# An S4D block with a gated feed-forward on one core: x kept on chip and normalised whole, gates folded into the magnitudes, the skip term added outside PE

## The chip, the cores and the metric

The kernel runs on one core of one Trainium2 chip. The metric is the device time of one execution in microseconds (us). Engines: PE multiplies matrices (PEld is its weight load), DVE, ACT and POOL work on vectors, SP issues the transfers. Each engine executes its own instructions strictly in order.

## The reference, cut to what matters

```python
L, D, N, F = 2048, 640, 128, 1728
mod = (silu(c) @ w_mod).reshape(c.shape[0], 6, 1, -1)
sa, ca, ga, sb, cb, gb = mod[:, 0], ..., mod[:, 5]
h = layernorm(x) * (1 + ca) + sa
dt = exp(log_dt); A = -exp(log_A_real) + 1j * A_imag
C = (C_real + 1j * C_imag) * dt[:, None]
K = 2.0 * einsum("dn,dnl->dl", C, exp((A * dt[:, None])[:, :, None] * arange(L))).real
y = irfft(rfft(h.T, 2 * L) * rfft(K, 2 * L))[:, :L].T + h * D_skip
x = x + ga * y
h = layernorm(x) * (1 + cb) + sb
x = x + gb * ((silu(h @ w1) * (h @ w3)) @ w2)
```

All is float32. The first half makes for each of 640 channels a convolution kernel of 2048 points out of 128 decaying oscillations, and convolves the normalised, modulated h with it by transforms. The second half is a gated feed-forward network.

## The kernel before, in words

The 640 channels are five blocks of 128 (b), each of eight chunks of 16 channels. For each of the forty chunks POOL adds phases (ph) from two small integer tables p and multiplies magnitudes (yy and xx out of e and x_e); ACT takes sines (tr); DVE makes five products of them (yy<-yy,tr and xx<-tr,xx, one of them 1024 wide); PE multiplies yy and xx into kps, which holds the convolution kernel of the chunk; ACT copies kps into ks (the rows). The tables p and step are begun twice per block, from pS, by `begin`: a shift by 0 to 4 bits into five places, on DVE for the very first, on POOL as a copy and four additions for the nine others. `al8` and `mag` prepare the exponentials per block; each may run on POOL or DVE.

The state h takes another way. x is loaded whole once (tiles xs) for its means and squares, then again in 64 KB pieces (xq), 128 channels by 4 rows of tokens at a time. `h_norm` scales and shifts such a piece into a PSUM tile hn (four instructions, on ACT or DVE), `h_mul` multiplies by the gate row rA, `h_add` adds rB and writes hb (both DVE, 512 wide), `h_store` sends hb to the scratch hs in HBM, and `h_fetch` brings it back turned, as xb. `fold` makes rA = (1+ca)*ga and rB = sa*ga out of the modulation rows rw. So ga is multiplied into h.

Both go through the same two transforms: the first on PE (ps<-wk,xb is h, task hh; ps<-wk,ks is the kernel, task k), copied to sp by ACT or DVE; the second, fh and fk, with the factors wb (2 MB); then DVE and ACT multiply the spectra (hq, fp, fk), PE makes the inverse transform fz, and zt is stored to zd. For blocks 1 to 4 the kernel's first transform already goes in chunk pairs: matmuls of 64 rows by 64 columns, in the four quadrants of the array. The skip term enters as the first matmul of each kps (kps<-dsk,ident). When all blocks are through, x and zd are gathered and the feed-forward part follows.

The order is written out by hand: every step is a task with a number, and `Plan.run` emits them in the order of the list ORDER, where a suffix a, d or p picks ACT, DVE or POOL for a task that leaves it open. Engines wait for each other by semaphores only. The line L147 in the profile is the helper that all of the first half is issued through; so its instructions are told apart by their tiles.

## Time and profile before

| what | us |
|---|---|
| median of 3 runs (lowest to highest) | 945.77 (945.37 to 947.55) |
| the profiled execution | 945.84 |
| its span, first to last instruction | 944.0 |
| PE busy, DVE busy | 849.6, 700.5 |
| ACT busy, POOL busy | 515.1, 346.4 |
| mean granted TensorE clock | 0.967 of full speed |

The span is what the profile resolves; 1.8 us lie around it. The busy times are sums over the whole span, and the first 376 us (the S4D half) and the rest (the feed-forward) have different limits, so the shares have to be read by stretch. A row of a group gives line, engine, operation, output<-inputs, sizes, count, then busy time in us, the mean in ns, and the idle time just ahead with what ended it.

### The profile page before, as it was taken

Reading aid. Unit: us, or ns where it says so; the run is one execution under the profiler, and the core shown is the slowest. Engines: PE = TensorE matmul, PEld = TensorE weight load, DVE = VectorE, ACT = ScalarE, POOL = GpSimd, SP = SyncE. Lnnn points to the kernel's source line nnn. Section 1 sums busy time; section 2 is a strip of 40 time slices with the busy share of each in tenths; the row PEclk is TensorE's granted clock in tenths of the full one; section 3 lists DMA queues with packets and bytes.
Section 4 is the critical chain, followed back from the end, with each engine's and each line's share of the span. In section 5 each row is a group of like instructions: output and inputs, shape, how many; then the busy total and the mean of one; then the engine's idle time right before and its main releaser. Section 6 shows DMA issues by size and latency. Waiting matters only on the chain.

```text
span 944.0 us, 22044 instructions
## 1 busy us (share of the span) xinstructions
PE 849.6 (90%) x8963; PEld 674.2 (71%) x8963; DVE 700.5 (74%) x1232; ACT 515.1 (55%) x886; POOL 346.4 (37%) x355
## 2 busy tenths in 40 slices
...
GB/s 244 241 255 126 170 147 170 48 104 103 27 124 40 177 149 232 254 182 153 151 64 146 84 161 77 111 84 70 42 84 70 57 50 48 38 77 111 77 149 82
DMA packets 124941, 112.78 MB, mean 119 GB/s; under 512 B 12328, under 2 KB 107048, under 8 KB 123560
## 3 DMA queue, kind: packets, MB, share of 16 engines
...
q10 hardware_dynamic: 768, 0.92, 0.4%
...
HBM read 90.38 MB, written 20.97 MB: 118 GB/s over the span
## 4 chain that ended last, share of the span: by engine, by line
PE 67%; DMA 10%; DVE 8%; ACT 6%; issue 3%; POOL 3%; SPq 1%; DVEq 0%; ACTq 0%; POOLq 0%
PE p L820 17%; PE acc L1067 16%; PE gu L1030 6%; PE gu L1032 6%; PE gu L1031 6%; PE ps L147 4%; PE fz L147 3%; DMA low<-zd 3%; PE kps L147 2%; PE fk L147 2%; DVE yy L147 2%; PE fh L147 2%; DVE fp L147 1%; DMA wq<-in_w 1%; ACT hn L147 1%
## 5 line engine op out<-in xcount | busy, mean ns | idle before, releaser
L1030 PE MATMUL gu<-xh,wh 128*128 128x512 f32 x270 | 106.2, 398 | 1.9 <-ACT xh L609 1.1
L1032 PE MATMUL gu<-xh,wl 128*128 128x512 f32 x270 | 105.4, 390 | 0.0
L1031 PE MATMUL gu<-xl,wh 128*128 128x512 f32 x270 | 105.2, 390 | 0.0
L147 ACT ACTIVATE tr<-ph 128x512 f32<-128x512 f32 (+1 forms) x160 | 92.9, 599 | 7.0 <-DVE yy L147 5.5
L839 POOL TENSOR_TENSOR ws<-wp 128x256 f32<-128x256 f32 x13 | 9.6, 739 | 230.9 <-DVE x L610 116.0
L147 POOL TENSOR_TENSOR ph<-p,p 128x1024 int32<-128x1024 int32 x40 | 78.2, 1955 | 3.0 <-ACT tr L147 2.7
L147 DVE TENSOR_TENSOR yy<-yy,tr 128x512 f32<-128x512 f32 (+1 forms) x80 | 75.4, 942 | 1.5 <-ACT tr L147 1.2
L723 ACT ACTIVATE wh<-wr 128x640 fp32r<-128x640 f32 x51 | 34.9, 731 | 70.5 <-PE gu L1031 55.6
L820 PE MATMUL p<-x,wch 128*128 128x512 f32 x208 | 68.3, 389 | 0.0
L1030 PEld LDWEIGHTS gu<-xh,wh 128*128 128x128 f32 x270 | 50.6, 188 | 18.3 <-issue 2.1
L147 PE MATMUL kps<-yy,xx 128*32 128x64 f32 x2560 | 49.3, 228 | 10.8 <-DVE xx L147 4.6
L1032 PEld LDWEIGHTS gu<-xh,wl 128*128 128x128 f32 x270 | 50.7, 188 | 11.2 <-DVE wl L733 0.4
L736 POOL MEMSET w2l<- 64x640 f32 x1 | 0.6, 631 | 157.8 <-PE acc L1067 157.8
L1031 PEld LDWEIGHTS gu<-xl,wh 128*128 128x128 f32 x270 | 50.7, 188 | 10.2 <-DVE xl L610 0.2
L147 DVE TENSOR_TENSOR xx<-tr,xx 128x512 f32<-128x512 f32 x80 | 54.3, 680 | 1.1 <-ACT tr L147 0.8
L857 DVE TENSOR_TENSOR s<-p,s 128x512 f32<-128x512 f32 x52 | 34.7, 682 | 27.0 <-ACT s L855 23.0
L147 POOL TENSOR_TENSOR yy<-e,e 128x512 f32<-128x512 f32 x48 | 52.7, 1109 | 4.5 <-PE kps L147 2.5
L147 PEld LDWEIGHTS kps<-yy,xx 128*32 128x32 f32 x2560 | 43.2, 113 | 11.6 <-POOL yy L147 4.5
L1045 DVE TENSOR_TENSOR a<-a,gu 128x512 f32<-128x512 f32 x26 | 17.8, 686 | 45.0 <-PE gu L1032 44.9
L1043 ACT ACTIVATE th<-gu 128x512 f32<-128x512 f32 x26 | 15.5, 596 | 64.3 <-PE gu L1032 64.3
L147 PE MATMUL ps<-wk,xb 128*64 128x128 f32 x640 | 47.1, 296 | 3.0 <-ACT sp L147 1.4
L147 PE MATMUL fh<-sp,wb 128*64 128x128 f32 x640 | 44.4, 284 | 4.9 <-DVE fp L147 2.2
...
## 6 DMA issues: line engine op xcount, KB each, us to landing
...
```

Source lines behind the costliest of these rows:

```text
L147: self.prev = self.k.order(f(*a, **kw), self.prev)
L723: self.nc.scalar.activation(wh[:, i], raw[:, i], AF.Copy)
L736: self.nc.gpsimd.memset(w2l[64:].bitcast(F32), 0.0)
L820: nc.tensor.matmul(to, t[:, o], y[:, k], start=start and k == i == 0, stop=stop and (k, i) == (n - 1, 2), skip_group_check=True)
L839: G.tensor_tensor(s[0], a21, a22, op=ALU.add)
L857: add = lambda o, bk, s: V.tensor_tensor(o, bk, s, op=ALU.add)
L1030: nc.tensor.matmul(pg, wh[:, k, :], xh[:, k, :], start=(k == 0), stop=False)
L1031: nc.tensor.matmul(pg, wh[:, k, :], xl[:, k, :], start=False, stop=False)
L1032: nc.tensor.matmul(pg, wl[:, k, :], xh[:, k, :], start=False, stop=(k == KT - 1))
L1043: nc.scalar.activation(th, gu[0], AF.Tanh, scale=0.5)
L1045: nc.vector.tensor_mul(a, a, gu[1])
L1067: nc.tensor.matmul(acc[k], *two(a, w), start=(m == 0 and i == 0), stop=(m == 12 and i == 2))
```

## The change

x is loaded once, ahead of the gates' weights, and stays on chip. Sixteen ACT instructions of 640 elements normalise it in place of the 80 small ones (each of the four tiles goes into the tile of the one before; the first into sp). The squares of the statistics are written to scratch so that x survives. The 80 loads of x in pieces disappear, and eight stores of 256 KB or 1 MB stand in place of 20 of 256 KB.

The gates are split: B = sa/(1+ca) is added to the normalised x, and A = (1+ca)*ga is multiplied into the magnitudes mag and the skip row dsk of blocks 1 to 4, which scales the convolution kernel in place of h. Block 0, whose magnitudes are needed early, still has A multiplied into x (`am`), then A*B added (`aa`), 512 wide; the other four blocks get one 2048-wide addition per tile of x (`ab`). Small column operations (`gates`) make A and B, and `gm`, `gd` multiply A into mag and dsk.

The skip matmuls disappear; ten `skip_add` instructions add dsk to the last column of ks. The first transform of h goes in chunk pairs too (`pair_tasks`): 64x64 quadrants. All ten `begin` are on DVE. The second half of w_mod is loaded in turn into the tiles of xb, wb and xs, and the load of the factors wb waits until these are used. In ORDER nearly all numbers change, since the tasks are others; three al8, mag and the like change engine there.

```diff
-1 2 8 7 12 78 80 3 79 86 81 41 14 19 82 20 42 84 21 15 83 43 85 16 153p 44 17 4 22 154 18 23 28 61 45 59 30 120 31 46 121 24
...
+1 2 5 78 3 80 4 6 81 20 14 82 19 41 84 21 7 15 42 8 22 83 16 9 11 190d 10 23 191 43 17 44 24 18 25 28 45 109 30 59 26 31 46 29
...
-            nc.scalar.activation(xs[:, j], xs[:, j], AF.Square, bias=self.h_nm[:, s], accum_out=self.h_ss[:, s])
+            nc.scalar.activation(self.rw[:, 0], xs[:, j], AF.Square, bias=self.h_nm[:, s], accum_out=self.h_ss[:, s])
...
-        def begin(e):
+        def begin():
 
             by = by_t(pS)
-            to = (p1[:, :, :, 1], by_t(st[:, 0]), by_t(st[:, 1]), p2[:, :, :, 1], by_t(st[:, 2]))
-            for i, d in enumerate(to):
-                if e == "DVE":
-                    V.tensor_scalar(d, by, i, None, op0=ALU.logical_shift_left)
-                elif i:
-                    add(d, to[i - 1], to[i - 1])
-                else:
-                    G.tensor_copy(d, by)
+            for i, d in enumerate((p1[:, :, :, 1], by_t(st[:, 0]), by_t(st[:, 1]), p2[:, :, :, 1], by_t(st[:, 2]))):
+                V.tensor_scalar(d, by, i, None, op0=ALU.logical_shift_left)
 
...
-        return [("DVE", .9, lambda: begin("DVE")) if b == h == 0 else ("POOL", 1.9, lambda: begin("POOL")),
+        return [("DVE", .9, begin),
...
-            b, c = d0 // P, d0 % P // C
-            last = kps.rearrange("p (e b) -> p e b", b=64)[:, :, 63]
-            for q in range(4):
-                s = slice(32 * q, 32 * q + 32)
-                nc.tensor.matmul(last[s], self.ident[:, s], self.dsk[:, b, 4 * c:4 * c + 4], start=True, stop=False,
-                                 tile_position=(0, 32 * q), skip_group_check=True)
...
-                                         start=False, stop=(r == 1), tile_position=(0, 32 * q), skip_group_check=True)
+                                         start=(r == 0), stop=(r == 1), tile_position=(0, 32 * q), skip_group_check=True)
...
-        plan.add("inv", None, 0, inv, ["cols", "mag1"], 0)
+        self.later = [f"k0.{x}.m" for x in range(6)] + ["colsf"]
+        self.stored = [f"{x}{i}" for x in ("as", "at") for i in range(4)]
+        plan.add("inv", None, 0, inv, ["cols", "mag1"] + self.stored, 0)
...
-            self.first_tasks(b, 0)
-            self.first_tasks(b, 1)
+            self.pair_tasks(b, 0)
+            self.pair_tasks(b, 1) if b else self.first_tasks(b)
...
-    def h_norm(self, pc, b, out, e):
-        x = self.xq[pc, b]
-        self.xq[pc, b] = out = out.rearrange("p (j d) -> p j d", j=4)
+    def h_parts(self, b):
+
+        x = self.xn[b].rearrange("p (k a j i) -> p k a j i", k=NB, a=4, j=4)
+        row = lambda r, k: bc(r[:, k.start * P:k.stop * P].rearrange("p (a i) -> p a i", i=E4), 2, 4)
+        return x, row
+
+    def h_norm(self, xs, b, j):
+
+        x, _ = self.h_parts(b)
         rstd, nb = self.h_rs
-        for j in range(4):
-            s = slice(4 * b + j, 4 * b + j + 1)
-            if e == "DVE":
-                self.nc.vector.tensor_scalar(out[:, j], x[:, j], rstd[:, s], nb[:, s], op0=ALU.mult, op1=ALU.add)
-            else:
-                self.nc.scalar.activation(out[:, j], x[:, j], AF.Identity, scale=rstd[:, s], bias=nb[:, s])
-
-    def h_mul(self, pc, b):
-        x = self.xq[pc, b]
-        self.nc.vector.tensor_tensor(x, x, bc(self.rA[:, pc * P:pc * P + P], 1, 4), op=ALU.mult)
-
-    def h_add(self, pc, b):
-
-        x = self.xq.pop((pc, b))
-        hb = self.hb[pc, b] = self.ring(f"hb{pc}{b}").rearrange("p (a j i) -> p a j i", a=4, j=4)
-        self.nc.vector.tensor_tensor(hb, x.rearrange("p j (a i) -> p a j i", a=4),
-                                     bc(self.rB[:, pc * P:pc * P + P].rearrange("p (a i) -> p a i", a=4), 2, 4), op=ALU.add)
-
-    def h_store(self, pc, b):
-        hb = self.hb.pop((pc, b))
-        self.nc.sync.dma_start(self.hs[pc, :, :, :, b, :].rearrange("a g t c -> (g t) a c"),
-                               hb.rearrange("p a j i -> p a (j i)"))
+        s = slice(4 * b + j, 4 * b + j + 1)
+        self.nc.scalar.activation(x[:, :, :, j].rearrange("p k a i -> p (k a) i"), xs[:, j].rearrange("p (k i) -> p k i", i=E4),
+                                  AF.Identity, scale=rstd[:, s], bias=nb[:, s])
+
+    def h_row(self, b, k, r, op, e):
+
+        x, row = self.h_parts(b)
+        v = x[:, k].rearrange("p k a j i -> p (k a) j i")
+        self.eng(e).tensor_tensor(v, v, row(r, k), op=op)
+
+    def h_store(self, b, k):
+
+        x, _ = self.h_parts(b)
+        to = self.hs[k].rearrange("k a g t b c -> b (g t) (k a) c")[b]
+        self.nc.sync.dma_start(to, x[:, k].rearrange("p k a j i -> p (k a) (j i)"))
...
-            add(n + "p", "PE", 1.1, lambda c=c: ch[c][4](), [n + f"m{i}" for i in range(5)] + (["dsk"] if b == 0 else []), t + 3,
+            add(n + "p", "PE", 1.1, lambda c=c: ch[c][4](), [n + f"m{i}" for i in range(5)], t + 3,
...
+            if c % 4 == 3:
+                add(f"d{b}.{c // 4}", ("POOL", "DVE"), (.28, .15), lambda e, h=c // 4: self.skip_add(b, h, e), [f"{g}.{x}.r" for x in range(c - 3, c + 1)] + (["gd"] if b else ["dsk"]), t + 3, port=True)
+    def skip_add(self, b, h, e):
+
+        to = self.ks[b][h][:, :, 63]
+        self.eng(e).tensor_tensor(to, to, self.dsk[:, b, 16 * h:16 * h + 16], op=ALU.add)
...
-            add(n + "n", ("ACT", "DVE"), (1.95, .85), lambda e, i=i, place=place: self.h_norm(b, i, place(), e), ...
-            add(n + "x", "DVE", .61, lambda i=i: self.h_mul(b, i), [n + "n", "fold"], t + .1)
-            add(n + "a", "DVE", .61, lambda i=i: self.h_add(b, i), [n + "x"], t + .2, take=[("hz", 1)], give=[(bank, n + "n")])
...
-            add("h0.f", "SP", 0, lambda: self.h_fetch(0), old, W["h"](b, 4), dma=[262144] * 4)
+            add("h0.f", "SP", 0, lambda: self.h_fetch(0), [f"as{i}" for i in range(4)] + ["mc0", "turn1"], W["h"](b, 4), dma=[262144] * 4)
...
-    def kernel_tasks(self, b):
+    def pair_tasks(self, b, m):
...
-                x = self.ks[b][i // 2][:, 8 * i % 16 + e, :]
+                x = self.ks[b][i // 2][:, 8 * i % 16 + e, :] if m else xb[:, :, 8 * i + e]
...
+        g = ("hh", "k")[m]
         for i in range(4):
+            t = W[g](b, 2 * i)
+            n = f"{g}{b}.{i}."
+            if m:
+                after = [f"g{b}.{2 * i}.r", f"g{b}.{2 * i + 1}.r", f"d{b}.{i // 2}"]
+            else:
+                after = [f"h{b}.f"] + (["wk"] + [f"mr{x}" for x in range(4)] + self.later if b == 0 else [])
+            old = [f"w{b - 1}.{x}.{'fk'[m]}" for x in range(8)] if b else []
...
+        def turn_cols():
+            pv = mt[1] = ps.tile([P, 512], F32, name="pvm", tag="f", bufs=3)
+            for o in range(4):
+                nc.tensor.matmul(pv[:, o:16:4], mt[0][:, o * P:(o + 1) * P], self.ident[:, 0:P:32], start=True, stop=True)
+
+        def gates():
+
+            pv = mt[1]
+            sa, ca, ga = (pv[:, k * KT:k * KT + KT] for k in range(3))
+            z, A, B, q = pv[:, 16:16 + KT], ab[:, :KT], ab[:, KT:2 * KT], ab[:, 2 * KT:]
+            V.tensor_scalar(q, ca, 1.0, None, op0=ALU.add)
+            V.scalar_tensor_tensor(z, q, -1.0, q, op0=ALU.mult, op1=ALU.max)
+            V.tensor_scalar(z, z, 1e-18, 4e-18, op0=ALU.is_lt, op1=ALU.mult)
+            V.tensor_tensor(q, z, q, op=ALU.add)
+            V.tensor_mul(A, q, ga)
+            V.reciprocal(q, q)
+            V.tensor_mul(B, sa, q)
+            V.tensor_mul(B[:, :1], B[:, :1], A[:, :1])
...
-        def fold():
-            self.rA, self.rB = self.rows[1], self.rows[0]
-            V.scalar_tensor_tensor(self.rA, self.rA, 1.0, self.rows[2], op0=ALU.add, op1=ALU.mult)
-            V.tensor_mul(self.rB, self.rB, self.rows[2])
-        add("fold", "DVE", 1.6, fold, [f"rw{g}" for g in range(4)], 22, port=True)
...
+        squares = [f"sq{b}{j}" for b in range(4) if b not in W["stat_v"] for j in range(4)]
+        for g in range(3):
+            add(f"pr{g}", "PE", .9, lambda g=g: spread(g), ["vc"], 21, take=[("f2", 1)])
+            add(f"rw{g}", "ACT", .5, lambda g=g: keep(g), [f"pr{g}", "lat1", "pa4"] + squares, 21, give=[("f2", f"pr{g}")])
+        rows = [f"rw{g}" for g in range(3)]
+        self.xn = [spf[:, :2560]] + [None] * 3
+        first, rest = slice(0, 1), slice(1, NB)
+
+        def norm(b, j):
+            if b and j == 0:
+                self.xn[b] = xs[b - 1].rearrange("p j d -> p (j d)")
+            self.h_norm(xs[b], b, j)
+        for b in range(4):
+            for j in range(4):
+                after = ["hscale", f"x{b}"] + ([f"n{b - 1}.{x}" for x in range(4)] if b else [f"mr{x}" for x in range(4)])
+                add(f"n{b}.{j}", "ACT", .74, lambda b=b, j=j: norm(b, j), after + ([f"n{b}.0"] if j else []), 22)
+            n = [f"n{b}.{j}" for j in range(4)] + rows
+            add(f"am{b}", ("POOL", "DVE"), (1.02, .6), lambda e, b=b: self.h_row(b, first, self.rA, ALU.mult, e), n, 22, port=True)
+            add(f"aa{b}", ("POOL", "DVE"), (1.02, .6), lambda e, b=b: self.h_row(b, first, self.rB, ALU.add, e), [f"am{b}"], 22, port=True)
+            add(f"as{b}", "SP", 0, lambda b=b: self.h_store(b, first), [f"aa{b}"], 22, dma=[262144])
+            add(f"ab{b}", ("POOL", "DVE"), (3.3, 2.25), lambda e, b=b: self.h_row(b, rest, self.rB, ALU.add, e), n, 22, port=True)
+            add(f"at{b}", "SP", 0, lambda b=b: self.h_store(b, rest), [f"ab{b}"], 22, dma=[262144] * 4)
+
+        def gate_sizes(e):
+
+            m = self.mag[:, 1:].rearrange("p b (e j) -> p b e j", j=4)
+            r = self.rA[:, P:].rearrange("p (b j e) -> p b e j", j=4, e=E4)
+            for k in range(NB - 1):
+                self.eng(e).tensor_tensor(m[:, k], m[:, k], r[:, k], op=ALU.mult)
+
+        def gate_skip(e):
+            for q in range(4):
+                s = slice(32 * q, 32 * q + 32)
+                d = self.dsk[s, 1:]
+                self.eng(e).tensor_tensor(d, d, self.rA[s, P:].rearrange("p (b q e) -> p b q e", q=4, e=E4)[:, :, q], op=ALU.mult)
+        add("gm", ("POOL", "DVE"), (1.5, 1.0), gate_sizes, ["q1.v3"] + rows, 22, port=True)
+        add("gd", ("POOL", "DVE"), (1.5, 1.0), gate_skip, ["dsk"] + rows, 22, port=True)
+        add("wb", "SP", 0, lambda: nc.sync.dma_start(self.wb, self.t_wb), rows + ["mr4", "lat1", "turn1", "mc3", "exp1"], 60, dma=[2097152])
...
-            w[k] = self.mod_load_rows(k, 1)
+            w[k] = (xbf, wbf, flat(xs[3]), wbf, flat(xs[3]))[k][:, :3 * D]
+            self.mod_load_rows(k, 1, w[k])
...
+            room = (["q0.t3", "q1.t3"], ["mr4"], [f"n3.{j}" for j in range(4)], ["mc1"], ["mc2"])[k]
+            add(f"c{k}", "SP", 0, lambda k=k: load_w(k), room + ([f"c{k - 1}"] if k else []), W["col"] + k, dma=[983040])
```

Three places show what moves. First DVE while the first half of block 0's chunks is made, around the fourth to sixth chunk. yy, xx with tr are the chunks' products; hn, hb the old h; sp and xs with rw the new additions and multiplications on x. Before:

```order
L147 TENSOR_SCALAR hn<-sp,rs_y_h,rs_n_h 128x128 x4
L147 TENSOR_TENSOR xx_520<-tr_48_621,xx_520 128x512
L147 TENSOR_TENSOR hn<-hn,rw 128x512 x2
L147 SCALAR_TENSOR_TENSOR yy_521<-yy_521,tr_48_619 128x16x32
L147 TENSOR_TENSOR hb_689<-hn,rw 128x512
L147 TENSOR_TENSOR yy_521<-yy_521,tr_48_619 128x16x32
L147 TENSOR_TENSOR hb_703<-hn,rw 128x512
L147 TENSOR_TENSOR yy_521<-yy_521,tr_48_699 128x1024
```

and now:

```order
L143 TENSOR_TENSOR sp<-sp,rw 128x512
L143 TENSOR_TENSOR xs_170<-xs_170,rw 128x512
L143 TENSOR_TENSOR xs_170<-xs_170,rw 128x2048
L143 TENSOR_SCALAR p_119<-pB 128x128
L143 SCALAR_TENSOR_TENSOR yy_602<-yy_602,tr_64_643 128x16x32
L143 TENSOR_TENSOR xx_601<-tr_64_652,xx_601 128x512
L143 TENSOR_TENSOR sp<-sp,rw 128x512
L143 TENSOR_TENSOR yy_491<-yy_491,tr_48_661 128x1024
L143 TENSOR_TENSOR xx_490<-tr_48_665,xx_490 128x512
L143 TENSOR_TENSOR xs_164<-xs_164,rw 128x2048
```

The old rows handle 128 channels of each tile of x; the new ones handle all 640 of a tile, among the products of the same chunks.

Second, the beginning of a table. On POOL before, between the preparation of two chunks:

```order
L147 TENSOR_TENSOR ph_1504<-p_123,p_124 128x1024
L147 COPY p_118<-pS 128x128
L147 TENSOR_TENSOR step<-p_118 128x64x2
L147 TENSOR_TENSOR step<-step 128x64x2
L147 TENSOR_TENSOR p_119<-step 128x128
L147 TENSOR_TENSOR step<-p_119 128x64x2
L147 TENSOR_TENSOR al_1513<-al,j_109 128x1024
```

and now on DVE, between chunk products and products of spectra (fp, fk):

```order
L143 TENSOR_TENSOR yy_1368<-yy_1368,tr_176_1412 128x16x32
L143 TENSOR_SCALAR p_118<-pS 128x128
L143 TENSOR_SCALAR step<-pS 128x64x2 x2
L143 TENSOR_SCALAR p_119<-pS 128x128
L143 TENSOR_SCALAR step<-pS 128x64x2
L143 TENSOR_TENSOR fp_1514<-fk_1294,hq 128x2x2x128
```

Five instructions change engine, and each now reads pS itself where POOL built one from the other.

Third, SP's queue ahead of the factors wb of the second transform. Before:

```order
L147 DMA hs<-hb_775 128x4x128
L147 DMA hs<-hb_778 128x4x128
L147 DMA xb<-hs 32x4x512 x4
L147 DMA xq_1047<-in_x 32x4x128 x4
L147 DMA xq_1052<-in_x 32x4x128 x4
L147 DMA wb<-in_t_wb 128x4096
L147 DMA xq_1113<-in_x 32x4x128 x4
```

and now:

```order
L143 DMA hs<-xs_170 128x4x128
L143 DMA hs<-xs_164 128x4x128
L143 DMA hs<-sp 128x16x128
L143 DMA xb<-hs 32x4x512 x4
L143 DMA hs<-xs_142 128x16x128
L143 DMA wb<-in_t_wb 128x4096
L143 DMA xb<-hs 32x4x512 x2
```

Of the old order only block 0's four stores stood ahead of wb; now all eight do, the last of them behind the last 2048-wide addition on DVE.

255 lines of the change are left out of this document (103 added, 152 removed).

## The prediction

> **What bounds the kernel now.** I read the table of stretches first, then the chain of waits, then the groups by operation and size, last the timeline around the places where work is added. In the stretches the columns are the limits in us, the length, then busy time and instructions of PE, PEld, DVE, ACT and POOL, PE clock, DMA share and GB/s.
>
> ```profile
> 0.00:20.00 20.00, 6.26 (x31) 3.67 (x31) 14.82 (x35) 9.28 (x15) 4.09 (x20) 1.00 0.92 252
> 20.00:97.00 77.00, 36.98 (x720) 24.21 (x722) 69.81 (x133) 66.03 (x135) 68.51 (x64) 0.73 0.80 206
> 97.00:324.00 227.00, 206.20 (x5055) 169.28 (x5054) 220.49 (x373) 203.69 (x367) 206.74 (x201) 0.98 0.39 107
> 324.00:376.00 52.00, 41.33 (x529) 25.72 (x529) 31.58 (x83) 16.40 (x28) 16.90 (x15) 0.93 0.71 194
> 376.00:944.00 568.00, 558.82 (x2634) 451.34 (x2632) 363.81 (x613) 219.75 (x345) 50.19 (x57) 1.00 0.37 101
> ```
>
> The last row is the feed-forward part: PE works 558.8 of 568 us, and the change touches none of it. So only the first 376 us are in play. There, from 97 to 324 us, DVE works 220.5 of 227 us (97%), PE 91%, POOL 91%, ACT 90%: DVE is the bound, three others follow within 21 us. The chain confirms only the last row (PE's 67% is mostly feed-forward):
>
> ```profile
> PE 67%; DMA 10%; DVE 8%; ACT 6%; issue 3%; POOL 3%; SPq 1%; DVEq 0%; ACTq 0%; POOLq 0%
> ```
>
> The pace of the chunks comes from the first and the last of the forty 1024-wide products of DVE:
>
> ```profile
> 48.45 1.21 DVE L147 TENSOR_TENSOR yy<-yy,tr 128x1024 f32<-128x1024 f32 x1
> ...
> ```
> ```profile
> 323.72 1.22 DVE L147 TENSOR_TENSOR yy<-yy,tr 128x1024 f32<-128x1024 f32 x1
> ```
>
> 275.3 us for 39 chunks is 7.06 us each. DVE's sum thus prices the change; PE's does not.
>
> **What leaves DVE.** Groups: line, engine, operation, out<-in, sizes, count, busy us, mean ns, idle before.
>
> ```profile
> L147 DVE COPY sp<-ps 128x512 f32<-128x512 f32 x27 | 18.0, 682 | 7.0 <-PE ps L147 7.0
> ...
> L147 DVE TENSOR_TENSOR hn<-hn,rw 128x512 f32<-128x512 f32 x20 | 13.7, 690 | 1.4 <-ACT hn L147 1.4
> L147 DVE TENSOR_TENSOR hb<-hn,rw 128x512 f32<-128x512 f32 x20 | 13.6, 682 | 0.1
> ...
> L147 DVE TENSOR_SCALAR hn<-xq,rs_y_h,rs_n_h 128x128 f32<-128x128 f32 x24 | 9.8, 412 | 1.0 <-ACT zt L147 0.3
> ...
> L147 DVE COPY zt<-fz 128x512 f32<-128x512 f32 x6 | 4.1, 678 | 0.0
> ...
> L147 DVE TENSOR_TENSOR rw<-rw,wb 128x640 f32<-128x640 f32 x1 | 1.7, 1686 | 0.0
> ...
> L147 DVE TENSOR_SCALAR hn<-sp,rs_y_h,rs_n_h 128x128 f32<-128x128 f32 x4 | 1.6, 410 | 0.1
> ```
>
> Norm, multiply and add of h: 9.8+1.6+13.7+13.6 = 38.7 us. Eleven of 27 sp copies and three of six zt copies go to ACT: 18.0×11/27 + 4.1/2 = 9.4. The fold of the gate rows: 1.7, and 0.8 from a row below: 2.5. Together 50.6 us. About 10.6 of it lies ahead of 97 us (block 0: four norms 1.6, eight products 5.5, the fold 2.5, a copy or two 1.0), 40 behind.
>
> **What comes to DVE.** Prices:
>
> ```profile
> L147 DVE TENSOR_TENSOR xx<-tr,xx 128x512 f32<-128x512 f32 x80 | 54.3, 680 | 1.1 <-ACT tr L147 0.8 <-POOL xx L147 0.2
> ...
> L147 DVE TENSOR_TENSOR yy<-yy,tr 128x1024 f32<-128x1024 f32 x40 | 48.4, 1210 | 1.5 <-ACT tr L147 1.2
> ...
> L147 POOL TENSOR_TENSOR step<-p 128x128 int32<-128x128 int32 x18 | 7.8, 431 | 1.4
> L147 POOL TENSOR_TENSOR al<-al,j 128x1024 f32<-128x1024 f32 x3 | 5.9, 1957 | 0.3 <-ACT x_e L147 0.3
> ...
> L147 DVE TENSOR_SCALAR p<-pB 128x128 int32<-128x128 int32 x4 | 3.5, 876 | 0.0
> ```
> ```profile
> 20.76 0.54 DVE L147 TENSOR_SCALAR p<-pS 128x128 int32<-128x128 int32 x1
> 21.16 0.41 DVE L147 TENSOR_SCALAR step<-pS 128x128 int32<-128x128 int32 x2
> 21.44 0.27 DVE L147 TENSOR_SCALAR p<-pS 128x128 int32<-128x128 int32 x1
> 21.58 0.26 DVE L147 TENSOR_SCALAR step<-pS 128x128 int32<-128x128 int32 x1
> ```
>
> A free table shift lasts 0.27 us. Nine more table starts of five shifts: 12.1; five more p<-pB: 1.4. A 512-wide operation 0.68, a 1024-wide one 1.21, so I estimate 1.21+2×0.53 = 2.27 for a 2048-wide one. Eight 512-wide operations on block 0: 5.4; four 2048-wide additions: 9.1; four al8 products: 4.8; three mag products: 2.0; the gates in magnitudes and skip row, seven skip additions and eight tiny gate operations, at 0.15 to 0.28 each: 4.9. Together 39.7. In the new order all eight 512-wide operations, three of the four 2048-wide additions, two table starts and two al8 products stand ahead of the eighth chunk's 1024-wide product, 19.5 us with the gates; 20.2 stand behind it. So DVE's own time rises by 19.5−10.6 = 8.9 in the front and falls by 40−20.2 = 19.8 behind it.
>
> **Waits that these bring.** Nearly all the added operations have all their data in SBUF; those removed read or write PSUM. That matters here:
>
> ```profile
> 283.25 1.07 POOL L147 TENSOR_TENSOR xx<-e,e 128x512 f32<-128x512 f32 x1
> 283.45 1.02 DVE L147 TENSOR_SCALAR p<-pB 128x128 int32<-128x128 int32 x1
> ```
> ```profile
> 67.45 0.81 DVE L147 SCALAR_TENSOR_TENSOR rw<-rw,wb 128x640 f32<-128x640 f32 x1
> 67.47 1.72 POOL L147 TENSOR_TENSOR yy<-e,e 128x512 f32<-128x512 f32 x1
> ...
> 68.19 1.69 DVE L147 TENSOR_TENSOR rw<-rw,wb 128x640 f32<-128x640 f32 x1
> 69.16 1.64 POOL L147 TENSOR_TENSOR xx<-e,e 128x512 f32<-128x512 f32 x1
> ```
>
> The shift at 283.45 ends 0.15 us after POOL's xx, though 0.27 is its free time: it waited for POOL. At 67 to 70 the two engines take turns. POOL's mean operation is 206.74/201 = 1.03 us; I estimate that POOL, some 24 us lighter, is busy 0.8 of the time, so a DVE operation that meets it at random waits 0.8×0.5 = 0.41 us. The four p<-pB rows measured 0.876−0.27 = 0.6. Bounds: nothing (POOL idle, as at 21 us) and a whole operation every time (the slower rival). I take 0.41 once per place (a run of neighbouring operations): 17 places in front, 7.0; 26 behind, 10.7. Behind such a wait on DVE stand the products of the next chunk; ACT's next sines wait for the banks that these set free, and POOL's next states for the buffers after PE's products, so a wait on DVE is paid in full as long as DVE is the bound.
>
> Behind the eighth chunk: −19.8+10.7 = −9.1, and I take a further 1 from the 6.5 us in which DVE idles, since those it waits for become lighter: **−10.1**, bounds −20 and +7 (the first rival below). In front: +8.9+7.0 = 15.9, of which 7.2 fit into DVE's idle time (77−69.8), and I take 4 as won because x is now loaded ahead of the gates' weights, so that its statistics come earlier (ACT's squares wait 4.1 us for them in a row below): **+4.7**, bounds 0 and +13.
>
> **What I cost at nothing.**
>
> ```profile
> L147 PE MATMUL ps<-wk,xb 128*64 128x128 f32 x640 | 47.1, 296 | 3.0 <-ACT sp L147 1.4 <-issue 0.8 <-DVE hb L147 0.5
> ...
> L147 PE MATMUL ps<-wk,ks 64*64 64x64 f32 x1024 | 19.5, 221 | 3.8 <-issue 3.3 <-ACT ks L147 0.5
> ...
> L147 ACT ACTIVATE sp<-ps 128x512 f32<-128x512 f32 x53 | 30.4, 591 | 9.3 <-PE ps L147 9.3
> ...
> L147 ACT ACTIVATE hn<-xq,rs_n_h,rs_y_h 128x128 f32<-128x128 f32 x40 | 18.5, 463 | 1.1
> ...
> L147 PE MATMUL kps<-dsk,ident 128*32 128x4 f32 x320 | 10.5, 183 | 1.3 <-ACT ks L147 1.3
> ...
> L147 ACT ACTIVATE xs<-xs,st_n 128x640 f32<-128x640 f32 x12 | 9.8, 817 | 4.1 <-DVE st_n L147 4.1
> ...
> L147 ACT ACT_TABLE_LOAD x11 | 14.1, 1283 | 0.9 <-PEq L1893 0.7
> ```
>
> State products in pairs: 47.1/5 = 9.4 us a block now; the kernel's own pairs take 19.5/4 = 4.9, so 22.6 us less PE; the skip products are up to 10.5 more. PE stands behind DVE; without that cover it is 33 us at most. ACT loses 40 norms of 18.5 us and twelve more at 0.46 (5.5), gets 16 of 640 elements (16×0.82 = 13.1), eleven copies and three zt (14×0.59 = 8.3) and two table loads (2.6): level, but some 7 us heavier in the front, where all 16 norms now stand and where it was busy 66 of 77; that is why the front's upper bound is +13. The skip addition puts a link between ACT's rows and the kernel's first transform, 0.2 us in every four chunks; PE has other work there, and bare it would be ten times 0.2. POOL loses nine table starts (5×0.43 = 2.2 us each), five p<-pB, four al8 (1.96 each) and three mag: some 33 us, which again only shortens waits. Eighty 64 KB loads and twelve stores leave SP's queue; DMA share was 0.39 in the stretch that they leave, so nothing is counted for them.
>
> Profiled time 945.84 + 4.7 − 10.1 = **940.4**; the median of the runs is 945.77, so no correction.
>
> **Rivals.** *Turn by turn (slower).* If, as at 67 to 70 us, each further operation of a run waits for a POOL operation, the nine starts have 36 further shifts and the gate products six: 42×0.8×1.03 = 34.6 us. POOL's own table addition, which needs the start, comes one to seven POOL operations later and then stands still, so I take half: 940.4+17, **957**. For it: those four rows. Against: the shifts at 21 us ran free, though POOL had little to do. It decides once a steady table start waits about 0.8 us more than I take. The Trainium skill, "SBUF — State Buffer", "Who interferes with whom", says that a DVE operation with two SBUF inputs, or a shift or copy in its fast mode, excludes GpSimd for a whole instruction and the other way round; the trace agrees (1.69 against 0.68), and it speaks for this rival.
>
> *The front eats it (no change).* The eighth chunk comes 10 us late, which the rows of 20 to 97 us allow, DVE (69.8 of 77) and ACT (66) both getting more there; against it stands that POOL, at 68.5, gets less: **945.7**.
>
> *All waits shrink (faster).* With POOL and PE both some 33 us lighter, meetings could be rare; POOL's 91% speaks against it, since eight tenths remain: −19.8 whole, front 0: **926**.
>
> *Late table wb.* It holds the second transform's factors. Its load now stands on SP behind the last store of x, and so behind DVE's last wide addition, after the eighth chunk.
>
> ```profile
> 93.38 1.19 SPq L147 DMA_DIRECT2D wb<-in_t_wb  x1
> ```
> ```profile
> 108.95 1.13 PE L147 MATMUL fh<-sp,wb 128*64 128x128 f32 x16 [0.30 <-ACT sp L147]
> ```
>
> 15.6 us pass from its issue to the first second transform; issued at 105, the spectra begin at 121, 12 late. PE and DVE would have to catch up; if the lighter PE hides only a third, **949**. That the change misses its aim can be at PE: pairs issue twice as many matmuls, and at 296 ns each they would win nothing, but that is off the bound.
>
> **How the numbers follow.** Chances: forecast 0.37, all waits shrink 0.16, no change 0.19, turn by turn 0.18, late wb 0.10. The likeliest alone runs from 935 to 943. For 8 in 10 it must reach into both sides: 926 to 957. A change under 0.3% (2.8 us) cannot be told from none. Faster 0.53, same 0.19, slower 0.28.
>
> **What would show it.** The eighth 1024-wide product some 5 us later than before and the fortieth 5 us earlier, at about 318 us, so 6.75 us a chunk between them; ps<-wk,xb about 25 us; added DVE shifts of mean near 0.4. Shifts of mean over 0.7 us would prove turn by turn; a first fh beyond 118 us the late table; a feed-forward part other than 568 us would make the whole account wrong.

## The result, and the profile after

The changed kernel takes 986.15 us (median of 4 runs, 984.32 to 987.15), the kernel before, run beside it, 946.4 (945.37 to 947.55): 1.0417 times as long, with a 95% interval of 1.0398 to 1.0437. It is slower by some 40 us, far beyond the range's upper end of 957. The profiled execution took 987.15 us, its span is 985.4.

The chain of waits still names the feed-forward part first; DVE's share of it has risen from 8% to 12%:

```profile
PE 71%; DVE 12%; ACT 6%; issue 3%; DMA 3%; POOL 2%; SPq 1%; DVEq 0%; POOLq 0%; ACTq 0%
```

The steady part, from the 1024-wide product of DVE of the ninth chunk to that of the fortieth, in the kernel before and then in the changed one, columns as in the prediction (limits, length, then busy time and instructions of PE, PEld, DVE, ACT, POOL, PE clock, DMA share, GB/s):

```profile
104.00:324.00 220.00, 200.33 (x4921) 163.98 (x4920) 213.60 (x361) 196.79 (x353) 200.97 (x196) 0.98 0.38 102
129.00:359.00 230.00, 197.86 (x5201) 162.24 (x5202) 204.95 (x342) 184.43 (x322) 177.05 (x153) 0.94 0.26 70
```

For the same chunks DVE now works 205.0 us where it worked 213.6, PE 197.9 for 200.3, ACT 184.4 for 196.8, POOL 177.1 for 201.0. Every engine has more idle time than before, DVE too: in this part no engine's own work is what became longer. The granted TensorE clock is lower there, 0.94 for 0.98 (0.950 for 0.967 over the whole span); with the table starts back on POOL (experiment 1) it is 0.98 again. Whether the lower clock adds to the loss or only goes with the longer pauses, no run separates. Where the time went is read from three marks of the timeline, the 1024-wide products of the ninth chunk (the first of block 1) and of the fortieth, and the first matmul gu of the feed-forward part. After:

```profile
128.83 1.21 DVE L143 TENSOR_TENSOR yy<-yy,tr 128x1024 f32<-128x1024 f32 x1
...
359.24 1.22 DVE L143 TENSOR_TENSOR yy<-yy,tr 128x1024 f32<-128x1024 f32 x1
...
417.86 0.96 PE L992 MATMUL gu<-xh,wh 128*128 128x512 f32 x3 [1.31 <-ACT xh L571]
```

and before:

```profile
103.81 1.21 DVE L147 TENSOR_TENSOR yy<-yy,tr 128x1024 f32<-128x1024 f32 x1
...
374.57 0.96 PE L1030 MATMUL gu<-xh,wh 128*128 128x512 f32 x3 [1.12 <-ACT xh L609]
```

With the fortieth product of before at 323.72 this gives four pieces, which serve for all the runs below. "Behind" is gu minus the fortieth, the feed-forward part the span's end minus gu.

| us | to the ninth | ninth to fortieth | behind | feed-forward | span |
|---|---|---|---|---|---|
| before | 103.8 | 219.9 | 50.9 | 569.4 | 944.0 |
| after | 128.8 | 230.4 | 58.6 | 567.5 | 985.4 |
| difference | +25.0 | +10.5 | +7.8 | −1.9 | +41.4 |

So the front loses most, the steady middle loses where a gain of about 10 was forecast, and a third loss, behind the last chunk, was not in the account at all. In the front, other than in the middle, DVE also has more to do: 109.4 of the 128.8 us up to the ninth product, where it had 91.3 of 103.8. These marks are from one profiled execution of each kernel.

### The profile page after: what moved, and what is told of

Read it like the earlier page. It is cut to its first block, busy times and chain, and to the rows that moved or that the text cites. A ratio compares the mean times of both kernels' runs of the same rounds, so it can differ in the third digit from the quotient of the medians.

```text
span 985.4 us, 22443 instructions
## 1 busy us (share of the span) xinstructions
PE 859.4 (87%) x9303; PEld 682.5 (69%) x9303; DVE 709.2 (72%) x1240; ACT 517.1 (52%) x863; POOL 317.2 (32%) x301
## 4 chain that ended last, share of the span: by engine, by line
PE 71%; DVE 12%; ACT 6%; issue 3%; DMA 3%; POOL 2%; SPq 1%; DVEq 0%; POOLq 0%; ACTq 0%
PE acc L1029 17%; PE p L782 16%; PE gu L992 6%; PE gu L994 6%; PE gu L993 6%; PE ps L143 5%; PE kps L143 3%; PE fz L143 3%; DVE yy L143 3%; PE fk L143 2%; DMA xs<-in_x 2%; DVE fp L143 2%; PE fh L143 2%; DVE xx L143 2%; POOL yy L143 1%
## 5 line engine op out<-in xcount | busy, mean ns | idle before, releaser
L143 ACT ACTIVATE tr<-ph 128x512 f32<-128x512 int32 (+1 forms) x160 | 93.8, 602 | 22.8 <-DVE xx L143 10.3
L143 PE MATMUL kps<-yy,xx 128*32 128x64 f32 x2560 | 54.7, 244 | 29.4 <-DVE xx L143 18.3
L143 PEld LDWEIGHTS kps<-yy,xx 128*32 128x32 f32 x2560 | 47.9, 122 | 39.5 <-issue 19.7
L143 POOL TENSOR_TENSOR yy<-e,e 128x512 f32<-128x512 f32 x48 | 55.3, 1158 | 21.4 <-PE kps L143 14.9
L993 PEld LDWEIGHTS gu<-xl,wh 128*128 128x128 f32 x270 | 50.7, 188 | 10.2 <-DVE xl L572 0.2
L143 PE MATMUL ps<-wk,xb 64*64 64x64 f32 x1280 | 46.5, 294 | 9.8 <-DVE sp L143 4.6
L143 PEld LDWEIGHTS ps<-wk,xb 64*64 64x64 f32 x1280 | 43.5, 217 | 15.2 <-DVE sp L143 4.8
L1007 DVE TENSOR_TENSOR a<-a,gu 128x512 f32<-128x512 f32 x26 | 17.9, 687 | 46.5 <-PE gu L994 46.3
L143 PE MATMUL fk<-sp,wb 128*64 128x128 f32 x640 | 45.0, 287 | 6.5 <-DVE fp L143 5.1
```

The lines of the kernel that those rows point to most:

```text
L143: self.prev = self.k.order(f(*a, **kw), self.prev)
L993: nc.tensor.matmul(pg, wh[:, k, :], xl[:, k, :], start=False, stop=False)
L1007: nc.vector.tensor_mul(a, a, gu[1])
```

## The experiments

Every run is compared with the kernel before on the same chip; ratios carry their 95% interval. The names starting with b are edits of the kernel before, those with a edits of the changed one, those with c edits of a_begin_pool. The kernel before took 946.4 to 947.4 us in all these groups, so that times of different groups are also set against each other in us.

**1. The table starts.** The changed kernel with the nine later starts back on POOL, as they were:

```diff
-        return [("DVE", .9, begin),
+        return [("DVE", .9, lambda: begin("DVE")) if b == h == 0 else ("POOL", 1.9, lambda: begin("POOL")),
```

> The changed kernel with one part undone: the nine later table starts go back to POOL (a copy and four additions), all else and the order as changed. Turn by turn (each of the five shifts of a start on DVE waits for a POOL operation, and POOL for it): the 45 shifts last 0.5 to 0.7 us in place of 0.14, so some 20 us of DVE time and POOL's waits for the start go away and 20 us of POOL time come back: 966 to 974. Rival, the new order as such (engines wait for each other in its long chain, whatever the starts cost): 982 to 990, DVE's idle time rising by what its busy time loses.

Measured: 971.25 us, 1.0258 (1.0219 to 1.0297). Fifteen of the 40 us are the starts, as expected by turns: 5.3 of them up to the ninth product, 7.7 from there to the fortieth, some 2 behind it. The groups of the changed kernel show the shifts, whose mean was forecast near 0.4 us:

```profile
L143 DVE TENSOR_SCALAR step<-pS 128x128 int32<-128x128 int32 x30 | 18.8, 672 | 0.0
...
L143 DVE TENSOR_SCALAR p<-pS 128x128 int32<-128x128 int32 x20 | 10.4, 520 | 0.0
```

The timeline of the changed kernel shows what they do at their worst, first DVE, then POOL in the same time (start, length, engine, instruction):

```profile
149.68 0.92 DVE L143 TENSOR_SCALAR p<-pS 128x128 int32<-128x128 int32 x1
150.47 3.07 DVE L143 TENSOR_SCALAR step<-pS 128x128 int32<-128x128 int32 x2
153.40 1.15 DVE L143 TENSOR_SCALAR p<-pS 128x128 int32<-128x128 int32 x1
154.42 0.95 DVE L143 TENSOR_SCALAR step<-pS 128x128 int32<-128x128 int32 x1
```
```profile
148.51 1.94 POOL L143 TENSOR_TENSOR ph<-p,p 128x1024 int32<-128x1024 int32 x1
150.42 1.06 POOL L143 TENSOR_TENSOR xx<-x_e 128x512 f32<-128x512 f32 x1
151.45 1.94 POOL L143 TENSOR_TENSOR ph<-p,p 128x1024 int32<-128x1024 int32 x1
153.35 1.06 POOL L143 TENSOR_TENSOR yy<-x_e 128x512 f32<-128x512 f32 x1
154.38 0.85 POOL L143 TENSOR_TENSOR p<-p,step 128x256 int32<-128x256 int32 x1
```

Five shifts and five POOL operations go in turn: each of the shifts that can be told apart ends some 0.15 us after a POOL operation does (150.60 after 150.45, 155.37 after 155.23); the start takes 5.7 us, where the five shifts of a start that met no POOL operation took 0.8 (215.04 to 215.87). Four of the ten starts are stretched like this, to between 3.7 and 5.7 us, and together last 16 us longer than four free ones. That is the rival "turn by turn". Is the alternation all of it? To see, only the first of the five goes to DVE, four additions stay on POOL, in the new order and in the old one; and in the old order all ten starts go to DVE whole.

```diff
-                if e == "DVE":
+                if e == "DVE" or not i:
```

> The changed kernel with only the first of the five operations of the nine later table starts on DVE, the four additions back on POOL. All five on POOL: 971 us; all five on DVE: 986 us. If the turns of the shifts cost the 15 us: 972 to 976. If it is the handover, as in the old order: 982 to 988.

> The kernel before with only the first of the five operations of each table start on DVE, the four additions on POOL as before. All five on DVE cost 26 us (b_begin_dve). If that is the turns of the single shifts, each waiting for a POOL operation of 1.1 to 2 us: a fifth, 948 to 954. If it is the handover (POOL reaches the table before DVE, which is late in its own queue, has begun it): most of it stays, 962 to 972.

```diff
-        return [("DVE", .9, lambda: begin("DVE")) if b == h == 0 else ("POOL", 1.9, lambda: begin("POOL")),
+        return [("DVE", .9, lambda: begin("DVE")),
```

> The kernel before with this part alone: all ten table starts on DVE, the order unchanged. Turn by turn: 45 shifts at 0.5 to 0.7 us put 20 us on a DVE that is 97% busy, and POOL, 20 us lighter, does not help: 956 to 966. Rival, the order: a start on DVE costs little where the rest is as before: 944 to 950.

Measured: a_begin_one 974.08 us, 1.0276 (1.0244 to 1.0309); b_begin_one 971.62, 1.0249 (1.0209 to 1.0289); b_begin_dve 973.38, 1.0276 (1.0231 to 1.0321). In the new order one shift costs next to nothing beside a_begin_pool and five cost 15 us, as turns would have it. In the old order one shift costs 25 us and five cost 26, beyond the 956 to 966 us that turns were to give: my theory of turns falls there. The waits of POOL and the timeline of b_begin_one show the other cause (columns of the waits: who waits for whom, us in all, times, longest):

```profile
POOL step L147 <- DVE p L147: 30.1, 7, 10.1
```
```profile
225.83 1.06 POOL L147 TENSOR_TENSOR xx<-e,e 128x512 f32<-128x512 f32 x1
236.96 0.46 POOL L147 TENSOR_TENSOR step<-p 128x128 int32<-128x128 int32 x1 [10.07 <-DVE p L147]
```
```profile
236.59 0.29 DVE L147 TENSOR_SCALAR p<-pS 128x128 int32<-128x128 int32 x1
```

The shift itself lasts 0.29 us. But it stands in DVE's order where DVE arrives 10 us after POOL has come to the same place, and POOL, which was ahead, stands still until then. Seven such places cost POOL 30.1 us. A start on POOL needed nothing from DVE; moved, it becomes a handover between two queues, and its price is how far apart they are there, not how long it lasts. In a_begin_one the same wait sums to 13.4 us in nine places without a loss to see; POOL seems to have that much room in the new order.

**2. Products of tables on POOL.** Of a_begin_pool, ten more tasks (al8, mag, gate products) from DVE to POOL by their suffix in ORDER:

```diff
-190d 192d 434d 436d 677d 679d 922d 1163d 172d 173d
+190p 192p 434p 436p 677p 679p 922p 1163p 172p 173p
```

> As a_begin_pool, and also the al8 and mag products of blocks 0 to 3 and the gate products of magnitudes and skip row on POOL, as far as the change has them on DVE. Turn by turn: the run of fourteen DVE operations after the eighth chunk goes, the ninth chunk comes 6 to 8 us earlier, 960 to 968. Rival, the order: 980 to 992, since POOL gets 20 us more and the order was made for another split.

Measured: 974.91 us, 1.0288 (1.0237 to 1.0338); not told apart from a_begin_pool. Moving this work from DVE to POOL brought nothing: up to the ninth product DVE works 96.9 us in place of 101.3, but that product, expected 6 to 8 us earlier, comes 2.5 later (126.1).

**3. Does DVE's sum price the change?** The prediction rests on this. From the kernel before, h_mul is taken out (twenty products of 13.7 us on DVE; h isn't multiplied by its gate row):

```diff
-        self.nc.vector.tensor_tensor(x, x, bc(self.rA[:, pc * P:pc * P + P], 1, 4), op=ALU.mult)
+        pass
```

> The kernel before without the twenty products of h and the gate row rA (13.7 us of DVE, 16 of them in the steady part), so this factor is left out. If DVE's time sets the pace there, as the prediction had it: 934 to 938. Rival, the engines wait for each other round the loop of a chunk, and DVE time taken away leaves idle time: 941 to 946.

Measured: 943.24 us, 0.9961 (0.9939 to 0.9984). Of 13.7 us at most some 6 come back, by the median about 4. A DVE that is busy 97% of a stretch was thus not its bound in the sense of the sum: most of what is taken from it does not come back. The same question in the changed order, by leaving out the added work of one kind at a time, each time against a_begin_pool's 971.25:

```diff
 c_no_adds, in h_row:
-        self.eng(e).tensor_tensor(v, v, row(r, k), op=op)
+        return
 c_no_gates, in gate_sizes and gate_skip:
-                self.eng(e).tensor_tensor(m[:, k], m[:, k], r[:, k], op=ALU.mult)
+                pass
-                self.eng(e).tensor_tensor(d, d, self.rA[s, P:].rearrange("p (b q e) -> p b q e", q=4, e=E4)[:, :, q], op=ALU.mult)
+                pass
 c_no_norms, in h_norm:
-        self.nc.scalar.activation(x[:, :, :, j].rearrange("p k a i -> p (k a) i"), xs[:, j].rearrange("p (k i) -> p k i", i=E4),
-                                  AF.Identity, scale=rstd[:, s], bias=nb[:, s])
 c_no_skip, in skip_add:
-        self.eng(e).tensor_tensor(to, to, self.dsk[:, b, 16 * h:16 * h + 16], op=ALU.add)
+        return
 c_bare: all four
```

> The changed kernel with its nine later table starts on POOL (a_begin_pool, 971 us), and without the twelve wide operations on x (the product and the addition on block 0, the additions on blocks 1 to 4), so sa is left out of h, and (1+ca)*ga out of block 0's. If these operations, 16 us of DVE, make the front late: the eighth chunk's wide product comes at about 98 in place of 110 us, 957 to 961. Rival, the front is late because the gates come later in the chain and the sixteen norms hold ACT: 966 to 971.

> a_begin_pool (971 us) without the eight products of the gates into magnitudes and skip row, so blocks 1 to 4 lack this factor. They last 2.9 us in a run of DVE operations between the eighth and the ninth chunk, where other engines wait. If that run makes the ninth chunk late: 966 to 968. Rival, the wait is for cols and the transforms of h behind: 970 to 972.

> a_begin_pool (971 us) without the sixteen norms of x on ACT (14.2 us), so h is not normalised. If these, in one stretch of ACT's queue between 55 and 80 us, hold the sines of the chunks behind them and make the front late: the eighth chunk's wide product at 97 to 101 in place of 110 us and 957 to 963. Rival, the gates' chain and the transforms of h behind cols set the front's end: 967 to 971.

> a_begin_pool (971 us) without the ten skip additions, so the skip term is left out. If their place, on DVE's or POOL's queue between ACT's rows and the kernel's first transform, holds these queues up: 958 to 964. Rival, they cost only their own 0.2 to 0.9 us each: 967 to 971.

> a_begin_pool (971 us) without the skip additions, the sixteen norms, the twelve wide operations on x and the eight gate products, so h is the raw x and skip and gates are left out: all vector work that the change adds, but for the tables. If that work is what is left of the loss: 944 to 952. If it is the order, with the transforms of h beginning 25 us later: 960 to 968.

| | us | ratio | to the ninth | ninth to fortieth | behind |
|---|---|---|---|---|---|
| a_begin_pool | 971.25 | 1.0258 (1.0219 to 1.0297) | 123.6 | 222.7 | 56.5 |
| c_no_adds | 969.19 | 1.0233 (1.0192 to 1.0274) | 120.7 | 221.8 | 56.6 |
| c_no_gates | 971.27 | 1.0260 (1.0224 to 1.0296) | 121.6 | 223.0 | 57.5 |
| c_no_norms | 973.45 | 1.0267 (1.0218 to 1.0316) | 124.0 | 222.7 | 55.9 |
| c_no_skip | 972.20 | 1.0254 (1.0224 to 1.0283) | 124.2 | 219.3 | 54.9 |
| c_bare | 966.40 | 1.0201 (1.0181 to 1.0221) | 118.6 | 220.4 | 56.7 |

Each kind alone lies within a_begin_pool's interval, and all of them together cost 4.9 us, with intervals that just touch. What the change adds to the engines, once the starts are gone, is thus not the main part of what makes it slow: 20 us stay without it.

**4. The skip term.** The skip products of PE taken out of the kernel before, and, apart from that, put on DVE as the change does:

```diff
-                nc.tensor.matmul(last[s], self.ident[:, s], self.dsk[:, b, 4 * c:4 * c + 4], start=True, stop=False,
-                                 tile_position=(0, 32 * q), skip_group_check=True)
 b_skip_dve, after the fourth row of a half block:
+                V.tensor_tensor(to, to, self.dsk[:, b, 4 * c - 12:4 * c + 4], op=ALU.add)
```

> The kernel before without the skip products on PE, and without any addition in their place, so the skip term is left out: the most that the change could win there. 10.5 us of PE go. PE off the bound: 944 to 947; each product also shortens the way of a chunk by 0.26 us, at most: 936 to 940.

> The kernel before with this part alone: the skip products leave PE, ten additions of 128x16 on DVE follow each fourth row of the kernel tiles. Both theories: PE loses up to 10 us that is not on the bound, DVE gets ten operations of 0.2 to 0.7 us: 944 to 951.

Measured: b_no_skip 946.67 us, 0.9990 (0.9964 to 1.0016); b_skip_dve 959.08, 1.0125 (1.0085 to 1.0165). Ten microseconds less of PE win nothing, as forecast. Ten additions of 16 columns cost 12 us in the old order, which has no place made for them, where 944 to 951 us had been expected: there they have a mean of 1.02 us, 0.69 in the changed kernel, and in c_no_skip their absence brings nothing. In b_skip_dve the addition stands behind the first transform of some chunks, whose skip term is missing, so this run prices a badly placed addition and not the change's.

**5. The pairs.** Groups of the changed kernel, matmuls of the state's first transform and their weight loads:

```profile
L143 PE MATMUL ps<-wk,xb 64*64 64x64 f32 x1280 | 46.5, 294 | 9.8 <-DVE sp L143 4.6 <-DVE fp L143 2.2 <-ACT sp L143 1.5
...
L143 PE MATMUL ps<-wk,ks 64*64 64x64 f32 x1024 | 19.6, 221 | 5.8 <-DVE fp L143 4.9 <-POOL ks L143 0.3 <-issue 0.3
...
L143 PEld LDWEIGHTS ps<-wk,xb 64*64 64x64 f32 x1280 | 43.5, 217 | 15.2 <-DVE sp L143 4.8 <-DVE fp L143 3.1 <-issue 2.3
...
L143 PEld LDWEIGHTS ps<-wk,ks 64*64 64x64 f32 x1024 | 17.2, 135 | 10.7 <-DVE fp L143 3.5 <-POOL ks L143 1.9 <-issue 1.8
```

Same form, same size, but a load of h takes 217 ns and one of the kernel 135. A difference that the code shows: the kernel's weights lie next to each other in ks, those of h are every 32nd element of a row of xb. So only that is changed; the transform then reads other elements of xb than it should. Once in the new order, once in the old one (there with 4*i in place of 8*i):

```diff
-                x = self.ks[b][i // 2][:, 8 * i % 16 + e, :] if m else xb[:, :, 8 * i + e]
+                x = self.ks[b][i // 2][:, 8 * i % 16 + e, :] if m else self.xb[:, 64 * (8 * i + e):64 * (8 * i + e) + 64]
```

> a_begin_pool (971 us), the pairs of h's first transform reading 64 neighbouring elements of xb as weights, not every thirty-second one, so the transform mixes up channels. The kernel's own pairs, which read neighbours, take 221 ns a matmul, those of h 292. If the stride is why: 220 to 235 ns, PE loses 14 us or more; the time by PE off the bound 968 to 972, by PE on it 957 to 963.

> The kernel before, the first transform of h reading 64 neighbouring elements of xb as weights, so the transform mixes up channels. In the changed kernel the same edit took 9 us. If PE is on the path only there: 943 to 947. If PE's weight loads bound the old kernel too: 934 to 940.

Measured: c_hh_flat 962.21 us, 1.0149 (1.0113 to 1.0184), 9 us below a_begin_pool; b_hh_flat 946.35, 0.9988 (0.9971 to 1.0006), nothing. The groups of c_hh_flat:

```profile
L143 PE MATMUL ps<-wk,xb 64*64 64x64 f32 x1280 | 26.4, 228 | 5.9 <-issue 2.9 <-ACT sp L143 1.4 <-DVE sp L143 0.8
...
L143 PEld LDWEIGHTS ps<-wk,xb 64*64 64x64 f32 x1280 | 23.1, 141 | 11.4 <-issue 4.6 <-ACT sp L143 1.9 <-DVE sp L143 1.7
```

The pairs then cost what was forecast for them, and the fortieth product comes 212.5 us after the ninth (336.25−123.72) in place of 222.7. Whom the slow loads held up is seen in ACT's wait for the first transforms from the ninth to the fortieth product, a_begin_pool first, c_hh_flat behind it:

```profile
ACT sp L143 <- PE ps L143: 16.3, 14, 2.7
```
```profile
ACT sp L143 <- PE ps L143: 6.5, 5, 2.5
```

In the kernel before the same wait is 8.0 us in nine places, with loads as slow, and 5.8 us in b_hh_flat: the old order seems to leave time for them, the new one doesn't.

**6. The order.** Two edits that change no work, only the list. In c_order four tasks of the front go to another place: the scale of the state and the first normalisation (125, 136) later, behind a product of the second chunk (235); an exponential (435) earlier, behind the last normalisation (164); the columns for the first transform (188) earlier, ahead of the gate products (172d). In c_drain three loads of the earlier blocks' zd on SP (1430 to 1432) go earlier, behind the store 1407 and ahead of the last two stores of zd.

```diff
 c_order:
-67 227 125
+67 227
...
-233 124 136
+233 124
...
-204 235
+204 235 125 136
...
-165 164
+165 164 435
...
-162 297 435
+162 297
...
-336d 171 172d
+336d 171 188 172d
...
-444 359a 188
+444 359a
 c_drain:
-1405 1407
+1405 1407 1430 1431 1432
...
-1390 1388 1430 1423 1431 1432
+1390 1388 1423
```

> a_begin_pool (971 us) with four steps of the front at other places, no work changed: the chain of small DVE operations for the norm's scale (7 us) behind four products of the second chunk, not ahead of them; the first norm behind it; block 1's exponentials on ACT (6 us with their table loads) behind the last norm, not amid the sixth chunk; cols ahead of the gate products. If the order of the front causes its lateness: the ninth wide product 4 to 8 us earlier than 123.6, and 964 to 969. If the front's lateness is elsewhere (loads of the gates' weights, PE): within 2 us of 971.

> a_begin_pool (971 us) with one change of order: the three last loads of zd's earlier blocks stand on SP ahead of the last stores of zd, as they did in the kernel before, not behind them. From the fortieth wide product to the first feed-forward matmul it takes 56.4 us there and took 50.9 before. If the queue behind these stores is the cause: 966 to 968. Rival, the late last transforms: 970 to 972.

Measured: c_order 981.97 us, 1.0339 (1.0290 to 1.0388); c_drain 974.42, 1.0294 (1.0260 to 1.0328). c_order has its ninth product here:

```profile
132.24 1.21 DVE L166 TENSOR_TENSOR yy<-yy,tr 128x1024 f32<-128x1024 f32 x1
```

8.7 us later than a_begin_pool (123.55), and its span ends 10.5 later (980.7 against 970.2): what the front loses is not made up by the rest; 4 to 8 us earlier had been expected. ACT's waits in its front name the moved scale, one single wait of 8.3 us where a_begin_pool has 4.7:

```profile
ACT sp L166 <- DVE rs_n_h L166: 8.3, 1, 8.3
```

As four tasks moved at once, the run doesn't say what cols alone would have done. c_drain shortens the piece behind the last chunk from 56.5 to 54.0 us, and the feed-forward part then takes 572.1 for 567.5: nothing is won in all, where 966 to 968 us had been expected.

**7. Do the causes add?** c_bare and c_hh_flat in one:

> This is the changed kernel with nine table starts back on POOL, without the added normalisations, additions, gate products and skip additions, and with the state's first transform reading its weights next to each other instead of every 32nd element (so it transforms other elements than it should). Alone, leaving out the added work won 4.9 us and the flat weights 9.0 us against 971.25. If the two are separate costs, they add: about 957, and what is then left over the old kernel, some 10 us, is order alone. If they are covered by each other, the time stays near 962, and some 15 us are order. If order costs nothing by itself once both are gone, it comes to 947.

Measured: 955.73 us, 1.0091 (1.0068 to 1.0115). Within the noise they add: 971.25−4.9−9.0 would be 957.4. The ninth and the fortieth product and the first gu of this run, whose span is 953.6:

```profile
119.82 1.21 DVE L143 TENSOR_TENSOR yy<-yy,tr 128x1024 f32<-128x1024 f32 x1
...
328.35 1.21 DVE L143 TENSOR_TENSOR yy<-yy,tr 128x1024 f32<-128x1024 f32 x1
...
385.79 0.96 PE L998 MATMUL gu<-xh,wh 128*128 128x512 f32 x3 [1.40 <-ACT xh L577]
```

The pieces are 119.8, 208.5, 57.4 and 567.8 us, against 103.8, 219.9, 50.9 and 569.4 before. The middle is now 11.4 us shorter than before; the front (+16.0) and the piece behind (+6.6) stay about as late as in the other runs, without any of the added work. By elimination that is the order of what is left, with its loads and stores; no run undoes it.

In sum, 40 us are some 15 of the table starts, 9 of the strided weights, 5 of all the added arithmetic, and a rest of 9 (c_bare_flat against before) to 11 (by subtraction): 22 to 23 lost in front and behind, less a gain in the middle and 2 in the feed-forward part. The rest is a net sum. c_bare_flat lacks the added arithmetic, but also the 38.7 us of norm, product and addition on DVE that the kernel before still does; so the new order by itself may cost more than these 9 us, and no run says how much.

## Why the prediction was wrong, point by point

**"DVE's sum thus prices the change".** This step failed first. DVE was indeed relieved: from the ninth to the fortieth product it works 205.0 us in place of 213.6, yet the stretch is 10.5 us longer. Time taken from DVE did not come back as time: b_no_h_mul takes 13.7 us from it and wins about 4 in the old order, and in the new one c_bare takes 26 us from it up to the fortieth product and wins about 5. I read the 97% now as the state of four engines in close step, each with little slack; that fits these runs and b_no_skip, but is not itself tested. The −10.1 behind the eighth product and the +4.7 ahead of it were sums. By the same marks the front came out at +14.1, the stretch from the eighth to the fortieth at +21.4, and +7.8 followed behind it. "All waits shrink" fell with the same step, and "the front eats it" had a late front of 10 us, but no loss behind it.

**"What I cost at nothing": the pairs.** They were priced by the kernel's own pairs, at 22.6 us less PE. They took 46.5 us, not about 25 (47.1 before). The row of the kernel's pairs was the wrong one to take, since its weights are read next to each other; c_hh_flat gives 26.4 with such weights. The sentence that at 296 ns each they would win nothing was the right one, and "off the bound" was the wrong end to it: in the new order the strided weights cost 9 us (c_hh_flat), in the old one nothing (b_hh_flat).

**"0.41 us once per place".** A start was priced at 5×0.27+0.41 = 1.8 us. Ten of them take 29.2 us by the two rows of shifts, 2.9 each and up to 5.7. The wait is paid by each operation of the run, not once. The rival "turn by turn" had the mechanism and put it at 17 us; a_begin_pool gives 15. That the two are so close is partly luck: it took all nine starts at half of their waits, where four of the ten were stretched and the others hardly. Its mark, a mean over 0.7 us, was set too high, because not all shifts meet a busy POOL: those of the start at 71.11 took 0.52, 1.16, 2.04, 0.27 and 0.26 us. Its time, 957, stood on the forecast of 940, and so fell short by what else was wrong. What neither held is the handover (POOL's 30.1 us in b_begin_one). The rows behind the rival were also read a little too high: 1.69 us is a row of 640 columns, and its like of the same width took 0.81 at 67.45, not 0.68.

**The front, "+4.7, bounds 0 and +13".** The eighth product came 14.1 us late, just over the bound:

```profile
96.82 1.22 DVE L147 TENSOR_TENSOR yy<-yy,tr 128x1024 f32<-128x1024 f32 x1
```
```profile
110.96 1.22 DVE L143 TENSOR_TENSOR yy<-yy,tr 128x1024 f32<-128x1024 f32 x1
```

Of the terms, the earlier x did what it was to do: the last of ACT's squares ends 8.6 us sooner (48.6 against 57.2). What the sum left out is that the gates' weights, now behind x, come later: PE waits 10.2 us for them before its first product of the modulation, which starts at 36.4 and not at 17.2.

The ninth product, of which I had worked out nothing, came 25.0 late. Between the two stands a run of DVE in the changed kernel:

```profile
112.10 2.28 DVE L143 TENSOR_TENSOR xs<-xs,rw 128x2048 f32<-128x2048 f32 x1
115.05 0.18 DVE L143 TENSOR_TENSOR ks<-ks,dsk 128x16 f32<-128x16 f32 x1 [0.67 <-ACT ks L143]
115.15 1.27 DVE L143 TENSOR_TENSOR mag<-mag,rw 128x128 f32<-128x128 f32 x4
116.34 1.17 DVE L143 TENSOR_TENSOR dsk<-dsk,rw 32x128 f32<-32x128 f32 x4
117.53 0.69 DVE L143 TENSOR_TENSOR x_e<-x_e,mag 128x512 f32<-128x512 f32 x1
...
122.36 0.29 DVE L143 TENSOR_SCALAR cols<-pv 128x5 f32<-128x5 f32 x3
```
```profile
118.36 1.07 POOL L143 TENSOR_TENSOR xx<-x_e 128x512 f32<-128x512 f32 x1 [6.25 <-issue]
```

POOL stands still for 6.25 us until DVE has made x_e, which is in the queue behind the gates; the profile books the wait as "issue", but POOL's operation reads x_e, and starts 0.14 us after that is done. The rows left out are a table start, from 118.14 to 122.49. PE's first transform waits for cols, last in the row. Its data come from PE's pv, here before (with cols behind it) and after:

```profile
88.97 1.05 PE L147 MATMUL pv<-ident,mc 128*128 128x4 f32 x8
90.72 0.29 DVE L147 TENSOR_SCALAR cols<-pv 128x5 f32<-128x5 f32 x3
```
```profile
99.20 1.87 PE L143 MATMUL pv<-ident,mc 128*128 128x4 f32 x8 [2.83 <-ACT mc L143]
```

Before, DVE took pv 0.7 us after its end; in the changed kernel cols stands 21.3 us behind it in DVE's queue, and h's first transform begins at 124.7, where it began at 93.7. What this place alone costs no run shows. The wide addition has the length that I gave it (2.28; estimate 2.27). So the durations were right and their place in the queue was not looked at. This too is only a part: without the additions, gates and skip additions c_bare still comes 14.8 us late to its ninth product, and there cols is taken at 109.7. Which places of the new order make that is not settled; c_order shows that four moved tasks are enough to shift it by 9.

**"Behind the last chunk".** +7.8 us from the fortieth product to the feed-forward part was in no term. It is there in every run in the new order (54.0 to 58.7, against 50.9), with the work left out as well. Part of the stretch is work that came ahead of the fortieth product before: 112 of the 640 matmuls fh lie behind it, where 48 did, and PE is busy 45.5 us there for 39.9. Whether that, or the loads of zd that c_drain moved, makes the 7.8 us stays open.

**"Late table wb".** The spectra did come late, the first fh at 138.8, against 109.0 before and a mark of 118. But wb, issued at 114.9, landed 10.8 us later, and was not what fh waited for: the kernel's second transform fk, which reads wb too, runs 5.5 us ahead of it.

```profile
133.31 1.14 PE L143 MATMUL fk<-sp,wb 128*64 128x128 f32 x16
...
138.84 1.13 PE L143 MATMUL fh<-sp,wb 128*64 128x128 f32 x16
```

What fh needs besides is h's first transform, which began only at 124.7, after cols, and went on to 136.8. So the mark was reached for another reason than the rival's, and no run shows wb to have cost anything.

**What held.** The feed-forward part (569.4 and 567.5), the skip products worth nothing (b_no_skip), ACT's normalisations at nothing (c_no_norms), and the 2048-wide additions' length. The gain of ten behind the eighth product is not among them. c_hh_flat, with the starts on POOL, the pairs at their forecast price and all other added work in it, takes 226.5 us from the eighth product to the fortieth (109.74 to 336.25), and the kernel before 226.9; c_bare_flat gains 11.4 from the ninth on, but only 3.7 from the eighth, and has none of the added work.
